# Attention over inducing points with a two-layer block: another order of the last 760 plan tokens, and the last three groups' stores joined

## The chip, the cores and the metric

The kernel runs on one core of a Trainium2 chip. The metric is the device time of one execution in microseconds; three runs of the kernel before gave a median of 542.07 us (541.64 to 542.36).

## The reference

```python
# B, N, m, C = 4, 12480, 32, 128; inducing: (32, 128); d_ff = 2048; float32 in and out
def mab(q, kv):
    s = (q @ kv.transpose(0, 2, 1)) / sqrt(C)
    a = exp(s - s.max(-1, keepdims=True))
    a /= a.sum(-1, keepdims=True) + 1e-09
    return a @ kv

h = mab(I, x)            # 32 inducing points attend to 12480 rows, per batch
y = mab(x, h)            # each row attends to the 32 points
t = y.reshape(B * N, C) @ w_in                              # (49920, 2048)
g = maximum(t, 0) + alpha * minimum(t, 0)
out = g @ w_out                                             # (49920, 128)
```

## The kernel before

The rows of a batch are cut into 24 groups of 512 and a last one of 192; four batches give 100 groups, numbered 0 to 99. Since `y` is a weighted sum of 32 rows of `h`, the first layer is folded into `hW = h @ w_in`, which has only 32 rows. TensorE's array is used as four row tiles of 32 rows (`r` = 0 to 3), which work at the same time.

For a group there are three kinds of work on TensorE (all issued at L383):

- 16 **fills** (`fill`): 32 rows of `hW` times the weights `rep` of the group's tokens into a PSUM bank. Each is then evicted with a ReLU to bf16 (`gt`) by ScalarE (L750, ACT) or VectorE (L752, DVE). A group of 192 tokens has 8 fills of two matmuls each, evicted 384 columns wide.
- the **second** layer (`second`): 16 chunks of `gt` times `W1`, each either as four quarters, one per row tile, or as one **whole** matmul over all 128 rows. All accumulate in one bank.
- one `linear` matmul that opens that bank (`enter`).

When the last chunk is in, `finish` has VectorE transpose the bank into `ot` (L818), multiplies it by the softmax's reciprocal sums (`scaled`, L826, on POOL, that is GpSimd; on VectorE for the very end) and stores `ob`: four stores per group, one for each 32 of the 128 output columns, each 512 pieces of 128 bytes (L851). Their queue depends on `to_end`, the number of groups that end later: four on SyncE for 3, four on ScalarE for 2, mixed for 1 and 0, else all on GpSimd.

The order of everything on TensorE, and with it the order on the evicting engines, is written out by hand in the string `PLAN`, 8041 tokens. A letter `a` to `h` with a bank number is a fill: two letters per row tile, the first evicted by ScalarE, the second by VectorE (`a`, `b` for r = 0, up to `g`, `h` for r = 3). `w`, `x`, `y`, `z` are the next quarter of the second layer in row tile 0, 1, 2, 3; `v` is a whole matmul (for groups 97 to 99 alone); `l` and `m` with a bank open an accumulation for quarters and for whole ones; `s` stands for the remaining work between (scores, sums), with its banks. Instructions go to each engine in the order of the tokens (`pin` ties each to the one before on its engine). A bank is filled again only when it was evicted, and a chunk waits for its `gt`.

Before, the groups at the end finish in the order 95, 97, 98, 96, 99. The last of ScalarE's 78 evictions in the final 760 tokens stands 103 tokens before the end; the 48 whole matmuls stand in three runs of 16.

Of the kernel before, what the change touches and what calls it, by code (L numbers as in the profile page):

```python
# [200 lines left out]
b02h12c223a312s4h212b012a323c12313f413s23e01h112l2wg42d33w231w3e03w32d1w31we431w3f31w3e01w32w3d1  # L201
2w3c42w32wd3g02w132w12h1wc4232xa02h3xa523x23b4x23a1x23xl0w23wxxwf3g5xw3e4s1h5xe3wxe4w3xwf13xw23x
wxe3wh5x2w32wc43wyd13wyc6wg3ys5b4yya1d6ywya5yyg3xb43xy3ya1xyxh6yc53yxh3ya4x3xy3xb1xza6zl5xe7zwxf
3zwc4wzwf1zxwe6zwh7xwzc3wzxwg4d1wzxwe6xzwf7zwzc3ywywzd4ywzc1yzl6yxwg7yxg3wxywh4xywxya1xywxyh2a7x
ywxyb3xya4xywd1ywxe2wxzf7s342zf1xwzxwe3zxwf7zwc2zwyc4zwyd1zwyzyc3zyxb7zyxg2yxb4zyxza1yxzyxb3ze7x
zyxl2yxwg4yxwyxwg1yxwh3yxwxg7wf4xzwxe0zwze1wzywd3zywzyc7wzyd4wzyc0wzwf1zwyza3yza7xyzb4xyza0xzyxl
1zyxwyxwg3yxwh7xywg4yxwh0xywg5xwzxe3wxzwf7xzwxze4wxf5zwc0zwzd3yws745d0wzywyzc3b7yzyzxa4yzxl5yzxb
0yzxa3yzxwzxywxg7ywxg4ywyxh0wyg3xwyxwyxh7wxe6wxzf4wxze0wxze3wzwd7zywc6zywzywd4zyc0zyxb3zyxzya7xz
yb6xzya4xzyl0xzywxg3ywxzywxg7ywxyh6wxywg4xe3wxzwxf2zwxzwe7xzwe4d6zwyzwyd3zwyzc2wyzd7wyza6yzl4xyz
wxyg3b2xyzxwyza6xyzb7xyzwxyg3wxyg2wxyh6ywxwxwxe7zs312xzb7e6xzwf3xzwe2xzwzwc1zywd6yzwc7yzwd2yzwza  # L210
3yzyb1xyzxa6zyxl7zyxwh2yxa3yxzwyxwg6yxwg1yxwyxwh3yxwg2xwe6xwzf5xwzxwze1xwzf3c2wzwzywd6yzwc5yzyzd
1yzb3xyzxa2yzxa6yxzl5yxzwyxza1yxzwyxg2wyxh3wyxg6wyxwyxh1wxe0wxze2wxzwxf3zwze6wzywzyc0wzyd1wzywc2
zyd3l6zyxwzya0xzyb1xzywxzya2zxyzxwys3012xh4ywxg3ywxywh0xywg2xe1wxwzf4xwzxwe3zxwzf2xwzc0wzd1wyzwy
c4zyza3yzxb2yzxl0yzxwyzc1b4yzxwyzxa3yzxwyg2xwyxwh1yxg4wyxwyxg3wyd7wxwe2zxwf1zxwzxwe4zxwf3zc7wzc2
ywzyd1zyxzya4xzb3yxza7yxzyxb2zyxzl1yxg4wyxwh3yxwg7yxzwyxzwyc2ywxg4yxwf3xwze7xwzxwf2s5437wyzd2wyz
c5wyzwyzd4we3zwyzb7yza2yzxya5zxyb4zxyl3zxywxzf7a2xzywxzywxg5ywxg4ywxyh2wxg7wxwxzf5wxze6wxze4wxzw
zd2wzywzc7ywzd6ywzyc5za4yzb2xyzxyl7zxywzxyb6g5xywzxywzxya4xywg2xywh6xywxywg5xwf4xwze0xwzf2xwze6x
wzwzd5ywzc4ywzc0ywzyl6zd2wzyxwzyxzya4xzyb5xzya0xzywxg2ywxzywxywh4xywg5xywxyg0wxs2154wxe0zwxf2zwx
e1zxwze4d5zwzywd0zywc2zyl1yzxwyzxa5zyxb4zyxwyzc2b0yzxwyzxa5yxwzyxwg4yxwg2yxwh0yxwyxwg5xwf4xzwe3x
zwxzwf2c0zwzd5ywyzwyzc4l3yzwxzya2xzyb0xzywxe5zwd4yzwxzya2xzywxzya0xywxh5ywxg4ywxywxg2ywxh0wxe7zw  # L220
xf4zwxzwe5c2zwyzwd0yzl7ywzxya4xzf5wzxywyzc2b0yzxwyzxa4yzxb5yzxwzyc2wzyxs0452ywxg0f6wxg4ywxg5ywxh
2ywxs0d6we4zxwzxwze5xwzf2c0wzd4zyl6yxzwxyza5xyzb2xyzwc0yzwxyzb4xyza5xyzwxyza2xyzwxywg0xyh4wxyg5x
wys21045wxywxh2e1wxf4zwc5zwyzwyc0zwyd1zwyc2zyzb5xyza4xyzl0xyzwxyza1xf2zwxzywxf4g5wxyzwxyza1xzywx
yg2wxyg5wxyh4wxwxf1zwxe3zwzwc2yzwyd5wzyc4wzyzl3d1yzwxyza2xyzwxf5zwxe4zwxyzb1xyza2xywzxyzwc5ywxyg
4wxyg1b2xywxywxe5b7xzwe4xzwd2zwxe1zwd5zwyc7zwyzc4yb2zxyl1zxywzxya5h7yxwzyxwg4d2ywzywxza5yxzyb7xz
xywg4ywxzywxg2yxwe5wxf7wzxf4xzws2657wxzf2wzc4wzyd6wzyc7l5zywwzxywwwzxe2b4zxywwzxywa7h6xywwxzywwx
zwe2wb4xyzwxwzya7xzyl6xywxg2ywxyh4wxywg7xywxwf0c2zwyxzxwxyxh4wc7yzxwyxzxwxe2d0zwyxzxwyxzwc7f4zxw
yxzxwyc2zb0yxzxxyza7xyzb4xyzxya2zxyzl0xywg7xywxyh4ywyxe2zwxyzwyxyyh3we7xzwyxyzywyxe4h2wxyzwyxyyz
wyc7f3zwyzwyc4zwyd2zwyzwc7yzyb3zxya4zxyzxa2yzxl7yzxzwyzzxa3zf4zxzwzyzxzwzyg2xywh1xwyzxg3wyxzzwxz
ze4wzxf2wzxwe1zxwzf3c5wzywzyc4wzyd2wzyc1zwyb3zyza5xyzxyb4zxya2zxyl1xzywxze3xwyh5xwyg4xwyxwyg2xwy  # L230
h3s6452xzwf3xzwe6xzwe4xzwf2xzwc5zwzwyd3wzywd6zywc4zya2zyl5zyxwh3yxwzyxwg4yxb6zyxwzyxa2yzxwyxwyg3
xwyxh4ya6xwe2xwxzf0wxzwxe3zwxzf6wzc4wzywd2zywc0zyzya3zxb6yzxyl4zxywzc2b0yzxywzxya3zxywg6xywxyh2w
xywg0xyg3wxywh7xwe6xzwxzwf2xzwe0xzwd3zwyzc7wyzwyza6d2yzl0xyzwxyg3wd7yzwxyzwxe6zb2xyzwxyza3xyzwxy
a7xywh6xyg2wxywxyg3wxf1wxwzxe7wzxf2zwc6zwyzwd3yzc1yzxa7yzxb2yzxl6yzxwyzc3b1yzxwyzxwyg7xb2yzxwyzx
we3zwxyg1wxywxywxh7ys23517xwzf2xwze3xwzf7c5wzwzyc1wzyd2wzya3zyzyxb7zyxa5zyxb1zyxl2zyxwze3xwzyd7w
yxg5wyxzwyxg1wyxg3wyxh7wyxwxg5wxzf1wxze4wxzwzd3wzyc7wzyd5wzyc1l4zyxwzyxa3zf7xwzyxwze1xzb5yxzwyxz
a3yxzwyxg7wyxwh1yxa5yxwg3yxwyxh0wyxwe7xwzf5wc1zywzywd3zywc0zya7zyxb5zyxl1zyxwzyc3b0zyxwzyxwg7f5x
wzyxwzyxa3zf0xwzyxwg7yxwzyxwg5yxwf3xwe0zxwzxwze7wd6zywzywc5yzd0l3zwxe7zwxzyb6xzywc5yzwxyzxb0yzxa
7zyxwyh6xa5yzxwyzxwyg0xwyxwg7yxwyh5xws60275h6we0xwzxwzd2e5zyc7wzywzyd0l6zyxwzyxa5zyd2wzyxwg7yxwz
f0xwzyxa5zyxwh2yxwze7xwzyxwh0yxa5yzxwyxza2yxg7wxwzxf0wze5wzywd2zywc4zya7zyxzb0yxzl5yxzwyxg2b4yxz  # L240
wyxzwyc7h0wyxzwyxza2yxh4wyxzwyc7zwyxzwe0xwf2zxwzxe4wzxwzxe7wzd0wzywzc1yl4zd2ywzxya7zxywh0xywzc1y
wzyxb2zyxa7zyxwzyxa0zyxwg1yxwyxwh2yxwg7yxwxf0we3xzwf1xzwze2xwzwzc7wyzd0yl3zwyxzya2xh1ywxzxya7zxy
b0zxywzc2wyzd1wyzxa7yzwxyzwxyg0wxyh2xwyg1wxye7wxwxzf0s6127f0zxwe6zxwzd1we7zwyzc2yzxyb0zxyzxya6zy
xb7zyxa1zyxl2zyd0wzyxwg6yxwh7yxwzyc1wzyxwg0yxwh6xywxwe7xzwxe1zwxzwf0c5zwyzwd7yzwc6yzwd1yza0yzxl5
yzxwyzxa7f6zxwyzxwyg0xb1yzxwyzxa7yzxwyg6xwyh0xwyxg1wyxwe7xwzxf4wzxe6wzwzyd1wzyc0wzyd7wzya4zya6xz
yxzb1yxzl0yxzwyd7zwe4xzwyxzwe6xzwyxg1wyxwh4yxwyg7xwyxh6wyxa3xe1wzxwzf4xwze7wzywzd3ywzc6yl1zyxwh4
yxwg7yxwzyxb3zyc6wzyxwzyxa4h7yxwzyxwzyd3a6zyxwzyxwg4yxwzxe7wzxwzxb6s34273e6wzd4f7wzxe2wzxs3yc6wz
# [60 lines left out]
def kernel(  # L308
# [815 lines left out]
```

## Time and profile before

| | |
|---|---|
| runs | 542.36, 541.64, 542.07 us; median 542.07 |
| profiled execution, first to last instruction | 540.4 us |
| median of the runs less that span | 1.7 us |
| busy: PE, DVE, ACT, POOL | 526.3, 504.2, 496.3, 394.7 us |
| mean granted TensorE clock | 0.996 |

The page gives the span of one profiled execution; the time of that execution outside its span is not on it, so times of the profile are set against the runs by these 1.7 us. PE is TensorE, DVE VectorE, ACT ScalarE, SP SyncE. Matmuls of different row tiles overlap, so that PE's busy time is that of at least one tile. Lines are those of the kernel before.

### The profile page before, as it was taken

The numbers are of one execution on the slowest core, as the hardware profiler recorded it, in microseconds if no ns is written. First come the engines' busy times: TensorE is split into PE (matmuls) and PEld (weight loads), VectorE is DVE, ScalarE is ACT, GpSimd is POOL, SyncE is SP. The second block draws the span as 40 slices with busy tenths as digits, with TensorE's granted clock in tenths as the row PEclk, the third lists the DMA queues.
The fourth block names the chain that finished last, engine by engine and source line by source line (L and its number), as shares of the span: only waits on it lengthen the run. The fifth ranks groups of instructions, "written<-read, shape, count | busy, mean of one in ns | idle before, by whom it ended". The sixth has DMA issues, their size and how long they took to land.

```text
span 540.4 us, 21603 instructions
## 1 busy us (share of the span) xinstructions
PE 526.3 (97%) x8988; PEld 332.7 (62%) x8988; DVE 504.2 (93%) x865; ACT 496.3 (92%) x994; POOL 394.7 (73%) x574
## 2 busy tenths in 40 slices
PE   4999999999999999999999999999999999999996
PEld 4655566566567566666667666666666566666653
DVE  3699999999989999999998999999999999999994
ACT  2499999999989999999999999999999999999950
POOL 5553778687667987687687987776767876776764
PEclk9999999999999999999999999999999999999998
DMA  8999999987799898887799797864354344334324
GB/s 197 212 186 139 182 185 156 170 142 113 112 175 149 134 160 152 162 129 145 117 153 166 117 164 158 168 101 113 66 93 113 66 96 112 70 89 108 68 42 85
DMA packets 114738, 71.12 MB, mean 132 GB/s; under 512 B 86784, under 2 KB 102784, under 8 KB 114640
## 3 DMA queue, kind: packets, MB, share of 16 engines
q0 software_dynamic: 19456, 38.62, 38.9%
q1 hardware_dynamic: 91984, 30.22, 32.9%
q8 instruction: 70, 1.15, 0.9%
q10 hardware_dynamic: 3200, 0.90, 0.7%
q14 instruction: 28, 0.23, 0.2%
HBM read 41.00 MB, written 28.95 MB: 129 GB/s over the span
## 4 chain that ended last, share of the span: by engine, by line
PE 90%; DMA 4%; DVE 2%; ACT 1%; POOL 1%; issue 1%; SPq 0%; POOLq 0%; DVEq 0%
PE bank L383 90%; DMA xn<-in_x_dram 2%; DMA rep<-e2d 1%; ACT gt L750 1%; DVE gt L752 1%; DMA e2d<-e 1%; POOL xn L412 0%; DVE ot L818 0%; PE bank L458 0%; ACT e L656 0%; DVE xT L461 0%; POOL ob L826 0%; DVE fr L608 0%; SPq L671 0%; POOL out_dram L851 0%
## 5 line engine op out<-in xcount | busy, mean ns | idle before, releaser
L383 PE MATMUL bank<-gt,W 32*128 32x512 bf16 (+1 forms) x6256 | 480.3, 371 | 0.1
L750 ACT ACTIVATE gt<-bank 128x512 bf16<-128x512 f32 (+1 forms) x906 | 464.5, 612 | 6.9 <-PE bank L383 4.6
L752 DVE TENSOR_SCALAR gt<-bank 128x512 bf16<-128x512 f32 (+1 forms) x662 | 417.7, 677 | 9.9 <-PE bank L383 6.1
L383 PE MATMUL bank<-rep,hW 32*128 32x512 bf16 (+1 forms) x1600 | 418.4, 368 | 1.5 <-DMA rep<-e2d 1.3
L383 PEld LDWEIGHTS <-W 32*128 32x128 bf16 x6256 | 264.4, 92 | 146.5 <-issue 46.6
L851 POOL DMA_DIRECT2D out_dram<-ob x386 | 247.3, 669 | 37.7 <-POOL ob L826 30.4
L826 POOL TENSOR_TENSOR ob<-ot,rdT 128x512 f32<-128x512 f32 (+2 forms) x99 | 106.3, 1074 | 93.8 <-DVE ot L818 79.5
L383 PEld LDWEIGHTS <-hW 32*128 32x128 bf16 x1600 | 136.9, 92 | 20.8 <-issue 5.1
L818 DVE STREAM_TRANSPOSE ot<-bank 128x512 f32<-128x512 f32 (+1 forms) x100 | 69.9, 699 | 6.7 <-PE bank L383 5.6
L383 PE MATMUL bank<-rep,hA 32*128 32x512 bf16 (+1 forms) x100 | 36.1, 367 | 0.0
L427 POOL DMA_DIRECT2D xn<-in_x_dram x32 | 20.7, 663 | 0.1
L481 ACT ACTIVATE e1t<-bank 128x256 bf16<-128x256 f32 (+2 forms) x14 | 5.0, 356 | 10.8 <-PE bank L383 10.8
L461 DVE COPY xT<-bank 128x1024 bf16<-128x1024 bf16 (+1 forms) x13 | 8.5, 650 | 4.9 <-PE bank L458 4.4
L383 PE MATMUL bank<-xT 32*128 32x512 bf16 x81 | 12.5, 376 | 0.0
L553 ACT ACTIVATE e<-bank 128x512 bf16<-128x512 f32 x18 | 11.0, 610 | 0.2 <-PE bank L383 0.2
L656 ACT ACTIVATE e<-bank 128x512 bf16<-128x512 f32 x18 | 11.1, 614 | 0.1
L383 PEld LDWEIGHTS <-xT 128*128 128x128 bf16 (+1 forms) x177 | 8.0, 97 | 4.1 <-issue 1.5
L383 PEld LDWEIGHTS <-hT 128*32 128x32 bf16 (+1 forms) x122 | 3.6, 93 | 11.0 <-issue 10.9
L383 PE MATMUL bank<-xT,hT 128*32 128x512 bf16 (+1 forms) x98 | 10.3, 388 | 0.0
L383 PEld LDWEIGHTS <-hA 32*128 32x128 bf16 x100 | 9.2, 92 | 1.8 <-issue 0.6
L458 PE MATMUL bank<-ident,xn 128*128 128x128 bf16 x96 | 9.0, 249 | 1.0 <-DVE xn L963 0.9
L412 POOL DMA_DIRECT2D xn<-in_x_dram x11 | 6.2, 583 | 3.3 <-DMA xn<-in_x_dram 2.5
(87 smaller groups left out, 131.7 us busy)
## 6 DMA issues: line engine op xcount, KB each, us to landing
out_dram<-ob POOLq DMA_DIRECT2D x373, 64.0 KB, 3.2
rep<-e2d SPq DMA_DIRECT2D x92, 128.0 KB, 3.2
xn<-in_x_dram POOLq DMA_DIRECT2D x37, 256.0 KB, 5.5
e2d<-e SPq DMA_DIRECT2D x24, 128.0 KB, 3.6
xn<-in_x_dram POOLq DMA_DIRECT2D x4, 512.0 KB, 8.2
rdT<-rt SPq DMA_DIRECT2D x96, 8.0 KB, 2.6
early<-in_moe_w_out_dram POOLq DMA_DIRECT2D x4, 256.0 KB, 10.6
xT<-xn SPq DMA_TRANSPOSE x36, 5.2
```

The source lines that it names most:

```text
L383: return pin(nc.tensor.matmul(o, lhsT, rhs, start=start, stop=stop, **kw))
L412: pin(nc.gpsimd.dma_start(out=xn[:, q0:q1, :], in_=src[:, q0:q1, :]))
L427: pin(nc.gpsimd.dma_start(out=st.xn[u][:, part, :], in_=src[:, part, :]))
L458: pin(nc.tensor.transpose(tp[:, k * P : (k + 1) * P], xn[:, q, j * C : (j + 1) * C], ident[:]))
L461: pin(nc.vector.tensor_copy(out=st.xT[:, u, qs[0] : qs[-1] + 1, :].rearrange("c q t -> c (q t)"), in_=tp[:, : len(qs) * GRP],))
L553: pin(nc.scalar.activation(out=e1[:], in_=ps[:], func=EXP, scale=scale, accum_out=st.es[:, u : u + 1]))
L656: pin(nc.scalar.activation(out=e2[:].rearrange("p (t j i) -> p t j i", j=n, i=32), in_=turned(ps[:pp, :w], n), func=EXP, scale=scale_of(st ...
L750: pin(nc.scalar.activation(out=gt[:, :w], in_=ps[:, :w], func=RELU))
L752: pin(nc.vector.tensor_relu(gt[:, :w], ps[:, :w]))
L818: pin(nc.vector.transpose(out=ot[:, :t], in_=acc[:, :t]))
L826: pin(engine.tensor_tensor(out=ob[:, k0 * w : k1 * w].rearrange("p (k m c) -> p k m c", k=k1 - k0, c=32), in0=ot[:, k0 * w : k1 * w].rearr ...
L851: pin(queue.dma_start(out=dst[a], in_=ob[32 * a : 32 * a + 32, :t].rearrange("p (b k) -> p b k", k=32),))
```

## The change

The first 7282 tokens keep their kinds and order; bank numbers differ in 1293 of them. The last 760 tokens stand in another order: 88 evictions are ScalarE's and 62 VectorE's (before 78 and 72), fills go on until 15 tokens before the end, and the whole matmuls are spread over 13 runs among the quarters. The number of matmuls of each kind is the same. The last groups finish in the order 94, 97, 95, 98, 96, 99.

`finish` stores differently for the last three groups (98, 96, 99; `to_end` 2, 1, 0). Group 98 has one store on ScalarE, group 99 one on SyncE. Group 96's first half is multiplied on GpSimd as before; its second half, on VectorE, and its two stores, on ScalarE and SyncE, are held back until group 99 has been multiplied and stored. The group with `to_end` 3 stores on GpSimd.

```diff
-        if to_end == 0:
-            scaled(nc.vector, 0, nb)
-        elif to_end == 1:
-            scaled(nc.gpsimd, 0, nb // 2)
-            scaled(nc.vector, nb // 2, nb)
-        else:
-            scaled(nc.gpsimd, 0, nb)
...
-        queues = {
-            3: (nc.sync,) * 4, 2: (nc.scalar,) * 4,
-            1: (nc.sync, nc.scalar, nc.gpsimd, nc.sync),
-            0: (nc.scalar, nc.gpsimd, nc.scalar, nc.sync),
-        }.get(to_end, (nc.gpsimd,) * 4)
-        for a, queue in enumerate(queues):
-            pin(queue.dma_start(
-                out=dst[a],
-                in_=ob[32 * a : 32 * a + 32, :t].rearrange("p (b k) -> p b k", k=32),
-            ))
...
+        def store(*queues):
+            n = NQ // len(queues)
+            for k, queue in enumerate(queues):
+                pin(queue.dma_start(
+                    out=dst[n * k : n * k + n],
+                    in_=ob[32 * n * k : 32 * n * (k + 1), :t].rearrange("p (b k) -> p b k", k=32),
+                ))
+
+        def rest():
+            scaled(nc.vector, nb // 2, nb)
+            store(nc.scalar, nc.sync)
+
+        if to_end == 0:
+            scaled(nc.vector, 0, nb)
+            store(nc.sync)
+            for fn in held:
+                fn()
+        elif to_end == 1:
+            scaled(nc.gpsimd, 0, nb // 2)
+            held.append(rest)
+        else:
+            scaled(nc.gpsimd, 0, nb)
+            store(*((nc.scalar,) if to_end == 2 else (nc.gpsimd,) * 4))
```

The address patterns of the stores in the built programs (partitions or outermost steps first, last number in elements of 4 bytes):

```
before, each quarter:        ob 32 x 16 x 32   ->  out 512 x 1 x 32   (group 99: 32 x 6 x 32 -> 192 x 1 x 32)
after, group 98 (ScalarE):   ob 128 x 16 x 32  ->  out 4 x 512 x 32
after, group 99 (SyncE):     ob 128 x 6 x 32   ->  out 4 x 192 x 32
after, group 96 (both):      ob 64 x 16 x 32   ->  out 2 x 512 x 32
```

The plan's end, from the first whole matmul on, before and after:

```
before  v*16 yd2m6h7yh1d5 v*16 zzd3m4zzzzzf2zzzzb7f1b5zzzzz v*16
after   vva6zyxxyyh4zzxxe2vvvf5xzzzxa4xa6vvb7yzzyyg2va4yyzc5yzh6vvvva2yzzzyyd7yh4vvc6zyzyzzyyvv
        m5zyzye7h2e4zvvvvvd6zzzze1f7vvvvc4zzzvvvc0h1b2zb6e7zg4vvvvm1zzzvvvve2zzzvvvvvvvvvvvv
```

More of the change, by code (lines that the diff above doesn't have):

```diff
@@ L206 @@
[L206 to L235, printed above, removed]
@@ L304 @@
+yywzzc2ywl0d1zwxyzxwze5yxzyb3yyzc2wxb1yxyzza5wzxyyd3zxzyxxa2wywyxwxwxyg1g5wxwh3s21zwzwxwxxe4zwf5e3wd
+2ywyyc1zyzyc4xyxzb5xyzl3xzwa2h1wxzxyyyxzyxwa4xyyzh5wwg2yxzwxxa1wzh4zxyzxe5yzxwwwxwwc2zze1ys4yzwwyd5z
+yc6wzzzywzyd2c4xh1xyxg5yyxzxyyxyza6zzxxxze2b4m1yg5vva6zyxxyyh4zzxxe2vvvf5xzzzxa4xa6vvb7yzzyyg2va4yyz
+c5yzh6vvvva2yzzzyyd7yh4vvc6zyzyzzyyvvm5zyzye7h2e4zvvvvvd6zzzze1f7vvvvc4zzzvvvc0h1b2zb6e7zg4vvvvm1zzz
+vvvve2zzzvvvvvvvvvvvv
 """
@@ L807 @@
     ended = [0]
+    held = []
     def finish(st, g, acc):
@@ L818, in finish @@
         pin(nc.vector.transpose(out=ot[:, :t], in_=acc[:, :t]))
-        ob = ob_pool.tile([P, GRP], f32, name="ob", tag="ob")
         to_end = B * NG - 1 - ended[0]
         ended[0] += 1
-        def scaled(engine, k0, k1):
-            w = t // nb
-            part = rbc[:, k0:k1]
-            pin(engine.tensor_tensor(
-                out=ob[:, k0 * w : k1 * w].rearrange("p (k m c) -> p k m c", k=k1 - k0, c=32),
-                in0=ot[:, k0 * w : k1 * w].rearrange("p (k m c) -> p k m c", k=k1 - k0, c=32),
-                in1=part, op=MULT,
-            ))
-        if to_end == 0:
-            scaled(nc.vector, 0, nb)
-        elif to_end == 1:
-            scaled(nc.gpsimd, 0, nb // 2)
-            scaled(nc.vector, nb // 2, nb)
-        else:
-            scaled(nc.gpsimd, 0, nb)
         t0 = st.b * N + s * SUP
@@ L844, in finish, with scaled @@
             dst = out[t0 : t0 + REM, :].rearrange("(i b) (a k) -> a i b k", b=t // 32, k=32)
-        queues = {
-            3: (nc.sync,) * 4, 2: (nc.scalar,) * 4,
-            1: (nc.sync, nc.scalar, nc.gpsimd, nc.sync),
-            0: (nc.scalar, nc.gpsimd, nc.scalar, nc.sync),
-        }.get(to_end, (nc.gpsimd,) * 4)
-        for a, queue in enumerate(queues):
-            pin(queue.dma_start(
-                out=dst[a],
-                in_=ob[32 * a : 32 * a + 32, :t].rearrange("p (b k) -> p b k", k=32),
-            ))
+        w = t // nb
+        ob = ob_pool.tile([P, GRP], f32, name="ob", tag="ob")
+        def scaled(engine, k0, k1):
+            pin(engine.tensor_tensor(
+                out=ob[:, k0 * w : k1 * w].rearrange("p (k m c) -> p k m c", k=k1 - k0, c=32),
+                in0=ot[:, k0 * w : k1 * w].rearrange("p (k m c) -> p k m c", k=k1 - k0, c=32),
+                in1=rbc[:, k0:k1], op=MULT,
+            ))
+        def store(*queues):
[19 more added lines that the diff above has]
+            store(*((nc.scalar,) if to_end == 2 else (nc.gpsimd,) * 4))
         st.rep.pop(g)
```

167 lines of the change are left out of this document (94 added, 73 removed).

## The prediction

> **What bounds the kernel now.** I read the page first, then busy time by stretches of the tail, then the timeline of each engine there, then the stores.
>
> ```profile
> span 540.4 us, 21603 instructions
> PE 526.3 (97%) x8988; PEld 332.7 (62%) x8988; DVE 504.2 (93%) x865; ACT 496.3 (92%) x994; POOL 394.7 (73%) x574
> ...
> ACT  2499999999989999999999999999999999999950
> ...
> q10 hardware_dynamic: 3200, 0.90, 0.7%
> ...
> PE 90%; DMA 4%; DVE 2%; ACT 1%; POOL 1%; issue 1%; SPq 0%; POOLq 0%; DVEq 0%
> ```
>
> ```profile
> 505.00:510.00 5.00, 5.00 (x90) 2.88 (x86) 4.85 (x9) 5.00 (x11) 2.91 (x5) 1.00 0.29 60
> 515.00:520.00 5.00, 5.00 (x69) 2.78 (x67) 5.00 (x9) 5.00 (x11) 3.02 (x6) 1.00 0.28 50
> 520.00:525.00 5.00, 5.00 (x36) 2.27 (x31) 4.46 (x8) 0.26 (x1) 2.36 (x4) 1.00 0.29 56
> 525.00:530.00 5.00, 5.00 (x37) 2.25 (x37) 3.42 (x7) 0.00 (x0) 4.28 (x6) 1.00 0.26 52
> 530.00:535.00 5.00, 5.00 (x34) 2.96 (x31) 3.60 (x7) 0.00 (x0) 1.94 (x2) 0.72 0.60 102
> 535.00:540.40 5.40, 0.75 (x5) 0.39 (x3) 0.74 (x2) 0.00 (x0) 1.19 (x2) 0.82 0.40 70
> ```
>
> Columns: stretch, length, then busy time and instructions of PE, PEld, DVE, ACT, POOL, then clock, DMA share, GB/s. Up to 520 DVE and ACT are full and PE too, but PE's 5.00 is a union over four row tiles and hides gaps in one of them. After 520 ACT does nothing, DVE evicts the last groups alone, and PE runs 36 matmuls in 5 us instead of 90: whole ones and lone ones. The span closes with 4.6 us in which PE is done and output travels. So the change works on some 20 us of PE tail and on that end.
>
> **The tail's sum.** Counted on the plan, both orders hold the same 150 fills, 548 quarter matmuls and 48 whole ones in the last 760 tokens. Before evicts 78 on ACT and 72 on DVE, after 88 and 62. The durations:
>
> ```profile
> 508.05 12.21 ACT L750 ACTIVATE gt<-bank 128x512 bf16<-128x512 f32 x24
> ...
> 501.73 0.72 DVE L818 STREAM_TRANSPOSE ot<-bank 128x512 f32<-128x512 f32 x1
> 502.37 5.18 DVE L752 TENSOR_SCALAR gt<-bank 128x512 bf16<-128x512 f32 x8
> 507.47 0.70 DVE L818 STREAM_TRANSPOSE ot<-bank 128x512 f32<-128x512 f32 x1
> ...
> 521.07 3.99 PE L383 MATMUL bank<-gt,W 32*128 32x512 bf16 x18
> ...
> 528.34 1.13 PE L383 MATMUL bank<-gt,W 128*128 128x512 bf16 x4
> ...
> 529.31 0.81 PE L383 MATMUL bank<-gt,W 32*128 32x512 bf16 x3
> 529.75 0.33 PE L383 MATMUL bank<-rep,hW 32*128 32x192 bf16 x2
> 529.96 1.02 PE L383 MATMUL bank<-gt,W 32*128 32x512 bf16 x4
> ...
> 532.49 3.27 PE L383 MATMUL bank<-gt,W 32*128 32x512 bf16 x17
> ...
> 479.30:533.20 53.90, 43.60 (x72) 0.99 0.34 71
> ```
>
> An ACT eviction takes 12.21/24 = 0.509 us; one of DVE (507.47 - 502.37)/8 = 0.6375, a transpose 0.64 to the next start. A matmul of 512 columns takes (3.99 - 0.37)/17 = 0.213 of its row tile, whole or quarter, one of 192 columns 0.08 by width. The last row says that DVE's last 72 evictions start at 479.3: the tail begins there, and its last matmul ends at 532.49 + 3.27 = 535.76, 56.5 us later.
>
> I add up each engine's work to a place in the plan. Before, at the 145th fill: DVE 67 evictions (62 full, 5 of 384 columns at 0.5) and 10 transposes, 48.7 us with its small ones; PE's fullest row tile 41.7 of its 49.8. Evictions lead by 7.0, so PE ends at 49.8 + 7.0 = 56.8; 56.5 was measured. After, at the 140th fill: ACT 41.7, DVE 43.4, PE 42.8. The widest lead is at the 120th: DVE 36.4 against 32.8, 3.6; PE in all 49.7. That gives 53.3, less the 0.3 by which this overshoots before: 53.0.
>
> Against it: the 48 whole matmuls stand in 3 runs before and 13 after. The row of four at 528.34 shows the price of leaving a run: 1.13 - 0.38 - 2 x 0.213 = 0.32 to the next start instead of 0.213, so 0.1; the way in is not separable in a row, I take 0.1 as well. Ten more runs cost 2.0 (bounds 0, where evictions are late anyway, and 2.0): 55.0. The plan's ragged places (four w, then four x) cost little: the fill at 529.75 stands in the plan behind seven z, of which one ended the row at 528.34 and three the row at 529.31; three follow only from 529.96. So PE lets a matmul overtake three of another row tile.
>
> **ACT's queue.** The store of group 98, the third from last, now stands in ACT's queue ahead of the last eviction of group 99, for which the last two whole matmuls wait. It waits for DVE's transpose and POOL's product:
>
> ```profile
> 525.91 2.57 POOL L851 DMA_DIRECT2D out_dram<-ob  x4 [0.30 <-POOL ob L826]
> ...
> 529.26 0.72 DVE L818 STREAM_TRANSPOSE ot<-bank 128x512 f32<-128x512 f32 x1 [1.41 <-PE bank L383]
> ...
> 530.06 1.07 POOL L826 TENSOR_TENSOR ob<-ot,rdT 128x512 f32<-128x512 f32 x1 [0.48 <-DVE ot L818]
> ...
> 535.86 0.38 DVE L818 STREAM_TRANSPOSE ot<-bank 128x192 f32<-128x192 f32 x1 [1.46 <-PE bank L383]
> 536.28 0.36 DVE L826 TENSOR_TENSOR ob<-ot,rdT 128x192 f32<-128x192 f32 x1
> ...
> L851 SPq DMA_DIRECT2D out_dram<-ob x7: 571/627/737, 529.6 to 536.7; - x7
> L851 ACTq DMA_DIRECT2D out_dram<-ob x7: 581/651/871, 531.2 to 537.3; - x7
> ...
> DMA to landing us min/median/max: 1.9/2.2/2.4
> ```
>
> From group 98's last whole matmul: 0.5 to the transpose, 0.72, 0.08, 1.07, 0.1, issue 0.65, eviction 0.45, so 3.6 us. PE meanwhile has six z (1.3), fourteen whole ones of 192 columns (1.1) and five switches (0.5): 2.9. The stall is 0.6 (0 if z run late; 2.6 if issuing four times the rows takes 4 x 0.65). PE ends at 479.3 + 55.0 + 0.6 = 534.9, 0.9 earlier. Bounds: 3.5 earlier with switches and stall hidden, 1.5 later. The half clock seen in the last stretches I leave as it is; gone, it gives back about 1 us, inside these bounds.
>
> POOL takes four more stores, group 97's, which SP issued before: product, gap and stores are 1.07 + 0.30 + 2.57 = 3.9, for groups 97 and 95 together 7.9 from 1.3 after group 97's end, so until 9.2; group 98's transpose is done 7.7 + 1.3 = 9.0 after that end (6.7 of matmuls on the fullest tile, five switched runs). POOL is free just in time; 0.2 more at worst lies inside the bounds.
>
> From there to the last issue: before 537.3 - 535.76 = 1.5. After: transpose, product of group 99, then DVE's half product of group 96, which now waits behind them (`held`), with gaps 1.35, and SP is busy with group 99's store to 1.5. Equal, nothing gained. Issues saved (12 stores become 4) cost nothing: SP and ACT had nothing else behind them.
>
> **The joined stores.** This decides.
>
> ```profile
> 530.50:531.00 0.50, 0.50 (x10) 0.31 (x8) 0.18 (x1) 0.00 (x0) 0.50 (x1) 1.00 0.01 2
> 531.00:531.50 0.50, 0.50 (x6) 0.21 (x3) 0.38 (x1) 0.00 (x0) 0.13 (x1) 1.00 0.75 130
> 532.50:533.00 0.50, 0.50 (x2) 0.00 (x0) 0.50 (x2) 0.00 (x0) 0.00 (x0) 0.50 1.22 198
> ...
> 539.00:540.40 1.40, 0.00 (x0) 0.00 (x0) 0.00 (x0) 0.00 (x0) 0.00 (x0) 0.50 0.02 3
> ...
> q10 hardware_dynamic: 3056, 0.38, 19.9%
> ...
> SPq L1119 <- DMA out_dram<-ob: 1.7, 2, 1.4
> ```
>
> A store of one quarter is 512 pieces of 128 B. Over 529 to 540.4 ACT's queue (q10) took 0.199 x 16 x 11.4 us for 3056 packets: 11.9 ns each on its engine. One queue alone moves 130 GB/s, 128 B per engine in 15.8 ns; two together 198, 10.3 ns. At 198 GB/s all sixteen engines must be at work. Every hardware transfer of this kernel has 16, 32, 96, 128, 192 or 512 as the outermost count of both its patterns; page q10's 3200 are 2944 pieces, 128 packets of the first load and 8 x 16 closing ones, so each was dealt over sixteen engines. The joined stores are the only ones with an outermost count of 4 (groups 98 and 99) or 2 (the two halves of group 96). If a transfer is dealt by its outermost count, these run on 4, 4, 2 and 2 engines. No row shows such a count, so the price is bounded: at least nothing (dealt over sixteen), at most everything on the same engines one after another. I take the latter's place, since a whole outermost step per engine is the plainest dealing that the rows allow, and there is no other reason for each to close with sixteen.
>
> The Trainium skill (DMA: Bandwidth & Descriptors, "Why a DMA increments its semaphore by 16 and not by 1") says that: the number of engines is the largest up to 16 that divides the outermost non-unit size of both patterns, and ScalarE's and SyncE's transfers take the lowest-numbered ones. By it the sum is the one below; no run here shows it yet.
>
> Per engine then: group 98 512 pieces, group 99 192, each half of group 96 512. If all share the first two engines, 1728. Group 98's last matmul is 3.6 before PE's end, its issue 2.5 after that, first pieces 1.4 after the issue (529.6 to 531.0 above): 534.9 - 3.6 + 2.5 + 1.4 = 535.2. ACT's queue is alone for 2.5 us (158 pieces at 15.8); then SP's 704 pieces and as many of ACT's alternate at 10.3 each, 14.5 us; the 162 left take 2.6. That is 19.6 us, to 554.8. From the last piece (539.1) to the end it was 1.3: span 556.1. The median lies 542.07 - 540.4 = 1.7 above the profiled span: 557.8. Bounds: all at 10.3, 17.8 us, with PE 2.6 earlier still, 553.4; all at 15.8, 27.3 us, 565.5.
>
> **Rivals.** (1) Few engines, but different ones for each store: the last store starts at 536.3 + 1.4 and takes 512 pieces at 11.9 to 15.8, 6.1 to 8.1: 546.8 to 548.8. For it: nothing in the rows says that engines repeat. (2) Faster: the joined stores are dealt over sixteen engines like the rest; then the end is as before and only PE's gain is left: 542.07 - 0.9 = 541.2, and 538.6 with the switches and the stall hidden. For it: all rows so far have sixteen. It decides as soon as group 98's store moves at 130 GB/s. (3) PE issues strictly in order: counted on the plan, a round opened whenever a row tile repeats, the tail takes 72 us after against 52 before, so 562 even with sixteen engines; the overtaking at 529.75 speaks against it.
>
> **How the numbers follow.** All few-engine stores on the same engines 0.62, rival 1 0.18, rival 2 0.18, rival 3 0.02. A change within 0.2% (1.1 us) can't be told from none. Rival 2's 538.6 to 543.6 falls 0.11 faster, 0.05 same, 0.02 slower. Predicted 557.8; the range 545 to 565 holds the first case and rival 1. Faster 0.11, same 0.05, slower 0.84.
>
> **What would show it.** Page part 3: q10 has 3072 + 128 pieces and 16 + 4 + 2 closings, 3222, by few engines, and 3248 by sixteen. The last fifteen microseconds show a DMA share near 2/16 and some 25 GB/s with all engines idle, and the chain's DMA share grows from 4% to about 7%. PE's last matmul lies at 534.9. ACT still evicts until about 532. Wrong would be a landing of the joined stores near 2.2 us, or a PE tail over 57.

## The result, and the profile after

The changed kernel takes 570.75 us (median of four, 569.65 to 571.71), before 541.86: ratio 1.0535, 95% interval [1.0517, 1.0553]. The forecast was 557.8 in 545 to 565: the right sign, and 13 us too little. The page of the changed kernel:

```profile
span 568.8 us, 21597 instructions
PE 534.8 (94%) x8985; PEld 331.5 (58%) x8988; DVE 502.0 (88%) x855; ACT 504.0 (89%) x1004; POOL 396.8 (70%) x576
...
ACT  2599999999999999999999999999999999888510
...
q10 hardware_dynamic: 3222, 0.92, 0.8%
...
PE 51%; POOL 25%; issue 12%; DMA 4%; DVE 1%; SPq 1%; ACT 1%; POOLq 0%; ACTq 0%; DVEq 0%
```

ACT's row ends in 888510 where before had 999950: in its last slices ScalarE is less full than before. q10 has the 3222 packets that were forecast for few engines. Stretches (length, busy time and instructions of PE, PEld, DVE, ACT, POOL, then clock, DMA share, GB/s):

```profile
505.00:510.00 5.00, 5.00 (x72) 2.73 (x70) 4.35 (x7) 4.60 (x10) 3.31 (x5) 1.00 0.26 54
515.00:520.00 5.00, 4.78 (x77) 3.34 (x79) 3.89 (x7) 4.32 (x10) 3.36 (x5) 1.00 0.33 66
...
530.00:535.00 5.00, 4.84 (x39) 1.52 (x36) 2.57 (x4) 2.19 (x4) 1.48 (x3) 1.00 0.27 56
...
545.00:550.00 5.00, 0.33 (x2) 0.10 (x1) 1.14 (x3) 0.49 (x1) 0.47 (x1) 0.83 0.21 32
550.00:555.00 5.00, 0.00 (x0) 0.00 (x0) 0.00 (x0) 0.00 (x0) 0.00 (x0) 0.50 0.37 41
555.00:560.00 5.00, 0.00 (x0) 0.00 (x0) 0.00 (x0) 0.00 (x0) 0.00 (x0) 0.50 0.21 22
560.00:565.00 5.00, 0.00 (x0) 0.00 (x0) 0.00 (x0) 0.00 (x0) 0.00 (x0) 0.50 0.21 22
```

Two things are to be seen. From 550 on every engine is idle and output trickles, at 41 and then at 22 GB/s: the joined stores, as forecast. But in 505 to 510 PE ran 72 matmuls where before ran 90, and ACT and DVE have gaps too. Nobody is full: they wait for each other. The end in the timeline (start, length, engine, line, then in brackets what the first of the group waited for):

```profile
541.22 2.57 POOL L838 DMA_DIRECT2D out_dram<-ob  x4 [0.96 <-POOL ob L829]
...
541.90 0.72 DVE L815 STREAM_TRANSPOSE ot<-bank 128x512 f32<-128x512 f32 x1
...
543.72 1.75 POOL L829 TENSOR_TENSOR ob<-ot,rdT 128x512 f32<-128x512 f32 x2
...
544.92 1.16 ACTq L838 DMA_DIRECT2D out_dram<-ob  x1
546.21 0.49 ACT L746 ACTIVATE gt<-bank 128x384 bf16<-128x384 f32 x1 [4.70 <-POOL ob L829]
546.75 0.33 PE L379 MATMUL bank<-gt,W 128*128 128x192 bf16 x2 [2.08 <-ACT gt L746]
```

PE's last matmul ends at 546.75 + 0.33 = 547.08 instead of 534.9. From there to the end of the span it is 21.8 us, forecast 21.2. So 12.2 of the 13 us of the miss lie in PE's tail.

To find it I cut that tail, from the start of its first fill, at the start of the last fill up to token 7900. Up to there lie 598 to 606 fills and quarters on the plan (600 before, 601 after; eight more or less are 0.4 us at 0.213 us for four), and the first whole one comes later. All profiles of the old order left as it was give 36.9 us for this **first part**, those of the new one 45.0, whatever else differs. The **second part** runs from there to PE's end. (The tail itself starts between 477.6 and 481.7 us in these profiles, whatever the order, so its length is compared and not its place.)

The last two columns are about waits. A **hand-over** is the place where a row tile begins its quarters of a group: all four row tiles add into one bank, and the first quarter of a row tile waits for the last one of the row tile before. How many tokens lie between a step and what it waits for I call its slack. The columns sum over the records of the first part: for each TensorE instruction with a semaphore wait, the time since the start of the TensorE instruction before it, as far as it is over 0.1 us; at the weight loads that wait for a hand-over, and at fills that wait for a bank.

```
order and stores                          first  second  hand-overs  fills
before                                     36.9    20.1      0.4      0.5
after                                      45.0    22.8      2.6      2.0
new order alone (e1)                       45.0    23.4      2.6      2.0
new order, row tiles alternating (e4)      42.6    23.1      2.9      3.8
new order, quarters and fills moved (e7)   39.1    23.6      0.3      1.2
  and group 98 stored by SyncE (e11)       39.1    19.5
new order, all mended (e10)                39.0    19.4      0.6      2.2
new order, five hand-overs wider (e9)      44.6    23.2      2.1      2.1
new order, no runs of three (e14)          43.9    23.6      1.0      1.8
new order, fills moved alone (e15)         42.4    23.9      1.3      2.6
old order made ragged (e5)                 39.6    18.5      0.9      3.1
old order, hand-overs tight (e12)          41.0    20.5      5.3      0.7
old order, runs of three (e13)             40.6    18.4      0.4      1.8
old order, evictions shared (e8)           36.9    20.3
```

### The profile page after: what moved, and what is told of

It is laid out like the page before. It is cut to its first block, busy times and chain, and to the rows that moved or that the text cites. A ratio compares the mean times of both kernels' runs of the same rounds, so it can differ in the third digit from the quotient of the medians.

```text
span 568.8 us, 21597 instructions
## 1 busy us (share of the span) xinstructions
PE 534.8 (94%) x8985; PEld 331.5 (58%) x8988; DVE 502.0 (88%) x855; ACT 504.0 (89%) x1004; POOL 396.8 (70%) x576
## 3 DMA queue, kind: packets, MB, share of 16 engines
q10 hardware_dynamic: 3222, 0.92, 0.8%
## 4 chain that ended last, share of the span: by engine, by line
PE 51%; POOL 25%; issue 12%; DMA 4%; DVE 1%; SPq 1%; ACT 1%; POOLq 0%; ACTq 0%; DVEq 0%
PE bank L379 51%; POOL out_dram L838 17%; POOL ob L829 8%; DMA xn<-in_x_dram 2%; DMA rep<-e2d 1%; DVE gt L748 1%; ACT gt L746 1%; DMA rdT<-rt 1%; SPq L667 0%; POOL xn L408 0%; SPq L707 0%; PE bank L454 0%; SPq L428 0%; DVE xT L457 0%; DVE fr L604 0%
## 5 line engine op out<-in xcount | busy, mean ns | idle before, releaser
L746 ACT ACTIVATE gt<-bank 128x512 bf16<-128x512 f32 (+1 forms) x916 | 471.9, 608 | 25.6 <-PE bank L379 17.7
L379 PE MATMUL bank<-gt,W 32*128 32x512 bf16 (+2 forms) x6253 | 488.2, 371 | 3.1 <-ACT gt L746 2.1
L423 POOL DMA_DIRECT2D xn<-in_x_dram x32 | 20.7, 663 | 0.1
L379 PE MATMUL bank<-xT,hT 128*32 128x512 bf16 (+1 forms) x98 | 10.3, 388 | 0.0
```

What stands on the lines that cost most here:

```text
L379: return pin(nc.tensor.matmul(o, lhsT, rhs, start=start, stop=stop, **kw))
L423: pin(nc.gpsimd.dma_start(out=st.xn[u][:, part, :], in_=src[:, part, :]))
L746: pin(nc.scalar.activation(out=gt[:, :w], in_=ps[:, :w], func=RELU))
```

## The experiments

**e1: the order alone.** Edit: the new `PLAN` in the kernel before, whose `finish` stays.

> The new order of the 760 tokens with the stores of before (four a group, queues by to_end as before). In the changed kernel PE's last matmul ends at 547.1 instead of 535.8 us and the end behind it takes 21.7 instead of 4.6 us. Theory: the two parts are separate; the order alone costs the 11 us of PE, 551 to 555 us. Rival: PE's delay is made by the joined stores (ScalarE held behind POOL and its store); then the order alone gives 541 to 545 us.

Measured: 554.2 us, ratio 1.0226 [1.0196, 1.0256]. Its tail is 68.4 us, its end 4.6 us behind PE as before. So the order alone costs 12 us where the forecast had it gain 0.9.

**e2: the stores alone.** Edit: the old `PLAN` with the new `finish`.

> The order of before with the new finish (joined stores, held half). Theory (joined stores run on 4, 4, 2 and 2 engines, the first ones each time): 557 to 561 us, q10 3222 packets, about 22 GB/s in the last stretches. Rival (the stores are late only because PE is late): 541 to 544 us.

Measured: 559.56 us, ratio 1.0325 [1.03, 1.0351]. PE ends at 533.3, the span at 557.7. The page's q10 and stretches of it:

```profile
q10 hardware_dynamic: 3222, 0.92, 0.8%
...
540.00:545.00 5.00, 0.00 (x0) 0.00 (x0) 0.00 (x0) 0.00 (x0) 0.00 (x0) 0.50 0.33 37
545.00:550.00 5.00, 0.00 (x0) 0.00 (x0) 0.00 (x0) 0.00 (x0) 0.00 (x0) 0.50 0.21 22
550.00:555.00 5.00, 0.00 (x0) 0.00 (x0) 0.00 (x0) 0.00 (x0) 0.00 (x0) 0.50 0.21 22
```

The same 22 GB/s without the new order. The two parts of the change nearly add: 2.3% and 3.3% against 5.4% together.

**e3: joining alone.** Edit to the changed kernel: four stores per group again, on the same queues.

```diff
-            for k, queue in enumerate(queues):
-                pin(queue.dma_start(
-                    out=dst[n * k : n * k + n],
+            for a in range(NQ):
+                pin(queues[a // n].dma_start(
+                    out=dst[a],
```

> The changed kernel with four separate stores per group (512 pieces each, outermost count 512 as before) on the same queues and in the same order as the changed kernel's joined ones, group 96's half still held back. If the joined access pattern is what costs (few engines), the end is again some 5 to 7 us behind PE and the time is that of the new order alone, 553 to 557. If the queues chosen or the held half cost, it stays at 563 to 571.

Measured: 559.1 us, ratio 1.0299 [1.0259, 1.0339], between the two expectations and some 2 to 6 us over what the first gave. Joining costs 1.0535 - 1.0299, or 2.4% (13 us); the choice of queues and the held half, together, are not free either: the span ends 7.7 us behind PE instead of 4.6. And four issues in ScalarE's queue hold the last eviction longer than one joined store does:

```profile
544.96 2.72 ACTq L838 DMA_DIRECT2D out_dram<-ob  x4
547.81 0.49 ACT L746 ACTIVATE gt<-bank 128x384 bf16<-128x384 f32 x1 [6.24 <-DMA out_dram<-ob]
548.35 0.48 PE L379 MATMUL bank<-gt,W 128*128 128x192 bf16 x2 [3.63 <-ACT gt L746]
```

3.63 us of stall instead of 2.08: here the joined issue gave back 1.5 us.

**e8: evictions shared, nothing else.** Edit: the old `PLAN`, seven of the last 15 evictions given to ScalarE by their letter (the lines show the fills alone).

```diff
-h5 h2 b6 d7 h1 b5 d2 h7 h1 d5 d3 f2 b7 f1 b5
+h5 g2 b6 c7 h1 a5 d2 g7 h1 c5 d3 e2 b7 e1 b5
```

> The old plan and the old stores; of the last 15 evictions, all VectorE's, every second one (7) is ScalarE's. It does alone what the change says of the evictions (both engines evict to the end). By the prediction's sum evictions led PE by 7.0 us there, and 7 x 0.64 = 4.5 us leave VectorE: 537 to 539. If PE's fullest row tile sets the end there (its matmuls with the closing linear ones are about 52 of the 56.5 us), nothing comes: 541 to 542.

Measured: 542.83 us, ratio 0.9999 [0.998, 1.0019]. Nothing comes. Its stretches show both engines at work from 520 on and neither full, while PE nearly is:

```profile
520.00:525.00 5.00, 4.84 (x45) 2.51 (x42) 4.30 (x8) 3.46 (x7) 3.85 (x6) 1.00 0.25 55
525.00:530.00 5.00, 5.00 (x32) 2.23 (x31) 1.76 (x3) 0.87 (x2) 4.12 (x6) 1.00 0.27 54
530.00:535.00 5.00, 5.00 (x34) 2.07 (x33) 2.36 (x5) 0.00 (x0) 1.07 (x1) 0.88 0.41 71
```

A stretch in which TensorE's clock is granted at 0.50 (the half clock below) falls into the second part before as well as here, with a mean of 0.92 and 0.91, so it hides no gain. These seven evictions were not late. The expectation's 52 us count the `linear` matmuls to the fullest row tile; but they open the banks, in row tile 0, and row tile 3 counts 49.8 us as in the prediction. What supports the expectation's argument is the second part: row tile 3 has 17 us of matmuls left there on the plan, and at full clock the old order takes 18.4 to 18.5 (e2, e5, e13), so little room is left for waiting.

**m1: TensorE by itself.** Edit: behind the end of the kernel before, bursts of matmuls are added: 96 quarters in runs of one to four and of eight per row tile; whole ones alone and in turn with four quarters; ten fills, each behind three quarters of three other row tiles, then ten behind four quarters of one, each with an eviction by ScalarE. Its time includes that added work.

> Kernel before with matmuls added behind its end, which nobody reads: 96 quarters in runs of 1, 2, 3, 4 and 8 per row tile (24 a tile, 5.1 us if the tiles overlap fully), whole ones alone and each followed by four quarters, and ten fills with an eviction on ScalarE, behind three quarters of other tiles or behind four of one tile. Theory A (TensorE issues nearly in the plan's order): the runs of 2, 3, 4 take about 10, 14 and 15 us. Theory B (it overtakes at least three, as a row of before showed): runs up to 3 take 5 to 6 us, runs of 4 up to 8, but an eviction behind four quarters of one tile starts 0.4 to 0.6 us later after its fill's start than one behind three different tiles, because it waits for the matmuls in front of the fill as well.

Measured, groups of instructions (busy time, mean ns of one) for runs of one (L1102), two (L1104), three (L1106), four (L1108) and eight (L1110), and whole ones alone (L1116):

```profile
L1110 PE MATMUL bank<-xT,W 32*128 32x512 bf16 x96 | 11.6, 375 | 0.0
...
L1108 PE MATMUL bank<-xT,W 32*128 32x512 bf16 x96 | 5.4, 374 | 0.0
L1102 PE MATMUL bank<-xT,W 32*128 32x512 bf16 x96 | 5.3, 374 | 0.0
L1104 PE MATMUL bank<-xT,W 32*128 32x512 bf16 x96 | 5.3, 374 | 0.0
L1106 PE MATMUL bank<-xT,W 32*128 32x512 bf16 x96 | 5.3, 374 | 0.0
...
L1116 PE MATMUL bank<-xT,W 128*128 128x512 bf16 x16 | 3.6, 380 | 0.0
```

Strictly in order, runs of four would take 24 x 3 x 0.2135 = 15.4 us. They take 5.4, hardly more than runs of one with 5.3: overtaking is free up to four deep, where no instruction waits, and at eight the time doubles. The Trainium skill (TensorE: Matmul & The Clock Gate, "Part 3: Packing small matmuls — row/col tiling") says that matmuls start and end strictly in program order; these starts do not. Whole ones alone follow one another at 0.216 us; four quarters and one whole matmul in turn had a period of 0.65 = 2 x 0.216 + 0.22, so a switch costs 0.11 each way, against 0.1 in the forecast. And the evictions:

```profile
579.76 0.37 PE L1140 MATMUL bank<-xT,W 32*128 32x512 bf16 x1
...
580.22 0.60 ACT L1141 ACTIVATE gt<-bank 128x512 bf16<-128x512 f32 x1 [61.13 <-PE bank L1132]
...
586.28 0.38 PE L1147 MATMUL bank<-xT,W 32*128 32x512 bf16 x1
...
587.36 0.60 ACT L1148 ACTIVATE gt<-bank 128x512 bf16<-128x512 f32 x1 [0.27 <-PE bank L1134]
```

Behind three quarters of three row tiles the eviction starts 0.46 us after its fill (L1140), behind four of one row tile 1.08 us (L1147), 0.62 later where 0.4 to 0.6 was expected: the fill overtakes three of the four, but its eviction waits until they are done too. The bracket names them, L1134, as what it waited for. In the records the last of the four and the fill count up the same semaphore, for whose value the eviction waits; whether a semaphore of its own would release it earlier, no run shows.

**e4: row tiles alternating.** Edit: tokens of the new order shifted within eight places so that row tiles take turns; stores of before.

```diff
- y y c7 y z w w d3 z z c5 x l1 y x z y z w d2 x y
+ z y w d3 y z w c5 y z x z l1 y x w z y d2 a7 z x
```

> The new order with only quarters and fills moved past one another within eight tokens, so that a row tile seldom repeats before the others had a turn: counted in strict order the tail takes 55 us of matmuls instead of 73 (54 before). Fills keep their order, engines and banks; whole matmuls stay where they are; stores of before. Theory (runs of one row tile in the plan cost the 11 us): 540 to 545 us, DVE and ACT full again until about 520. Rival (the spread whole matmuls and the later evictions cost it): 549 to 555 us.

Measured: 551.53 us, ratio 1.0179 [1.0153, 1.0205]. Only 2.7 us come back, which is in the rival's range. The rival's reason is not what is left, though: the first part ends ahead of the first whole matmul and still takes 5.7 us more than the old order's. It falls to 42.6, but its waits grow from 4.6 to 6.7 us: in moving tokens, I brought six hand-overs as near as 2 tokens and fills nearer to the evictions that free their banks.

**e5: the old order made ragged.** Edit: tokens 7282 to 7840 shifted by three places at most so that row tiles repeat.

```diff
- z y d1 w z y c2 z y x z b6 y x z a0 y x z l7 y x
+ c7 d1 y y w z z c2 x y y z z b6 a0 x x y z l7 z y
```

> The old plan and the old stores, with tokens 7282 to 7840 made as ragged as the new plan (row tiles repeat two and three at a time; the same count of rounds, 73 us against 54), each token moved by three places at most; hand-overs stay 4 to 5 tokens at the least. Theory R (raggedness): 8 to 12 us slower than before, 550 to 554. Theory S (slack): little is lost, since overtaking covers runs of up to four: 541.5 to 545.

Measured: 544.88 us, ratio 1.0039 [1.0015, 1.0062]; first part 39.6. That is theory S's range. Raggedness, mostly by twos, still costs 2.7 us in the first part, and the waits at fills grow by as much, 0.5 to 3.1. On the plan this order has as many strict rounds as the new one.

**e7: slack mended.** Edit: the new order with its quarters and fills moved against each other for distance; the fills keep their own order, banks and engines. (The whole matmuls came to stand in six runs by this, not in thirteen as the expectation has it.)

```diff
- y y c7 y z w w d3 z z c5 x l1 y x z y z w d2 x y
+ d3 c5 z z w y z y y z y x d2 z y a7 z x z l1 w y
```

> The new plan with the four-per-group stores of before (as in the run of the order alone, 554.2), in which only quarters of the last 760 tokens have moved against the fills and whole matmuls; the fills keep their order, banks and engines, the whole matmuls their 13-odd places. Every first quarter of a group in a row tile now stands at least 5 tokens behind the last one of the row tile before (2, 2, 3, 4, 4 at the least before the edit, 5 in the kernel before), and a fill stands further behind the use that frees its bank. The tokens stay ragged: opening a round whenever a row tile repeats counts 68 us of it (73 in the new plan, 54 in the old). Theory S (missing slack: the instruction that waits for a hand-over or for a bank holds up all four row tiles): nearly all of the 12.7 us comes back, 540 to 545. Theory R (raggedness or spread whole matmuls themselves cost): most stays, 550 to 554.

Measured: 548.89 us, ratio 1.0106 [1.0079, 1.0133]; between the two theories' ranges; first part 39.1, so 5.9 of its 8.1 us are back. Slack was not all that changed: from token 7282 to 7900 the same row tile still comes twice or more in a row at 85 places where the new order has 100, but three times or more at 4 where it has 23. The stretch 479 to 500 before, after and in e7:

```profile
479.00:500.00 21.00, 21.00 (x363) 13.09 (x360) 20.95 (x36) 20.99 (x42) 15.67 (x22) 1.00 0.36 86
```

```profile
479.00:500.00 21.00, 20.63 (x294) 10.40 (x292) 17.57 (x29) 17.50 (x34) 12.66 (x18) 1.00 0.31 72
```

```profile
479.00:500.00 21.00, 21.00 (x338) 13.62 (x334) 20.17 (x33) 19.93 (x39) 14.66 (x21) 1.00 0.36 84
```

363, 294 and 338 matmuls; DVE and ACT go from 17.5 back to 20. The second part did not shorten, which left the stall at the end as a suspect.

**e11: the store out of ScalarE's queue.** Edit to e7:

```diff
-            3: (nc.sync,) * 4, 2: (nc.scalar,) * 4,
+            3: (nc.sync,) * 4, 2: (nc.sync,) * 4,
```

> The new plan with the slack mended (548.9, ratio 1.0106), and group 98's four stores on SyncE instead of ScalarE; nothing else. If the last eviction queued behind these stores in ScalarE's queue holds TensorE up at the end (one wait of 2.8 us there), 2 to 3 us come back: ratio 1.005 to 1.007. If the last fills are late anyway, nothing: 1.010.

The waits, e7 ahead of e11 (total, times, longest):

```profile
ACT gt L746 <- DMA out_dram<-ob: 5.8, 1, 5.8
...
PE bank L379 <- ACT gt L746: 2.8, 1, 2.8
```

```profile
PE bank L379 <- issue: 0.3, 2, 0.2
```

PE's wait for ScalarE is gone, and the second part falls from 23.6 to 19.5 (some of that is e7's half clock behind the wait). But the time is 546.68 us, ratio 1.0104 [1.0076, 1.0132], no better than e7's: SyncE now issues 11 stores one after another, and the end comes 5.9 us behind PE instead of 4.7. In the time itself the expected 2 to 3 us cannot be shown: the profiled spans are 546.8 and 545.0.

**e9, e14, e15: which slack?** Three edits to the new order, each aimed at one thing. e9 widens the five tightest hand-overs to 5 tokens (15 tokens differ). e14 lets quarters trade places until no row tile comes three times in a row. e15 moves fills alone.

```diff
e9
- z w z z w x f2 y
+ z w x z z w f2 y
e14
- y y c7 y z w w d3 z z c5 x l1 y x z y z w d2 x y
+ y z c7 w z y w d3 y z c5 x l1 y y w x z z d2 y x
e15
- y y c7 y z w w d3 z z c5 x l1 y x z y z w d2 x y
+ x c5 y y y y z d2 w w z a7 z x l1 y x z y a3 z w
```

> The new plan with the stores of before (the order alone measured 1.0226 of before, 12.3 us), with one thing mended: quarters next to the five tightest hand-overs are shifted by one to three places, so that no first quarter stands nearer than 5 tokens behind the last one of the row tile before (2, 2, 3, 4, 4 before the edit); 15 tokens differ. If the tight hand-overs were most of the missing slack, the first part of the tail loses 3 to 6 us of its 8 and the time is 547 to 551. If the slack is missing between fills, evictions and banks, 0 to 1.5 us come back: 552.5 to 554.

> The new plan and the old stores; in tokens 7282 to 7900 quarters trade places among themselves so that no run of three or more of one row tile is left (23 before); the fills keep their places, and hand-overs are as near as they were (3, 3, 4, 4, 5 at the least). Theory Q: the tail's first part, 45.0 us in the new order, becomes 40.5 to 42, the time 549 to 552. Theory W: it stays within 1 us, 44 to 45 and 553 to 555.

> The new plan and the old stores; only fills move: 121 of the 150 in the last 760 tokens stand elsewhere among the quarters (2.2 tokens earlier on average), while the fills among themselves and the quarters and whole matmuls among themselves keep their order exactly. So hand-overs stay as near (2, 2, 3, 3, 4 at the least) and row tiles repeat as often. Theory F (the new order asks for banks too soon: a fill that waits for its bank holds everything behind it, and that delays the next eviction in turn): the tail's first part, 45.0 us in the new order, falls by 3 to 4.5 us, the time to 549 to 551.5. If hand-overs and runs of one row tile are what costs, at most 1 us comes back: 553 to 555.

Measured ratios: e9 1.0245 [1.0218, 1.0271], e14 1.022 [1.0202, 1.0238], e15 1.0163 [1.0116, 1.0209]. First parts: 44.6, 43.9, 42.4. The edits gave back 0.4, 1.1 (my theory had 3 to 4.5) and 2.6 (3 to 4.5 expected). None alone is the cause; their sum, 4.1, is short of the 5.9 that e7 recovers. Nor is each gain the price of the one thing named: without runs (e14) the waits at hand-overs fell as well, by 1.6, and with the fills moved (e15) the waits at fills grew, 2.0 to 2.6, while those at hand-overs fell, 2.6 to 1.3, and runs of three or more went from 23 to 15.

**e12, e13: the same put into the old order.** e12 draws 22 hand-overs closer, most to 2 or 3 tokens. e13 makes 26 runs of three or four by letting quarters trade places; every fill stays.

```diff
e12
- w z x f0 w z c7 w z y d1 w z y c2 z y x
+ w z x f0 y w z c7 w z d1 w z y c2 x z y
e13
- z y d1 w z y c2 z y x z b6 y x z a0 y x z l7 y x
+ w y d1 w z y c2 z z x y b6 x y y a0 x z z l7 z x
```

> The old plan and the old stores; only first quarters of a group in row tiles 1 to 3 are moved forward, so that 17 of the 26 hand-overs stand 2 or 3 tokens apart and 5 stand 4 or 5 (5 to 9 in the old plan). The rest keeps its order. If a tight hand-over stalls all row tiles for 0.15 to 0.25 us, 22 of them cost 2 to 5 us: 544 to 547. If hand-overs are covered by what row tiles still have queued, 541.5 to 542.5.

> The old plan and the old stores; in tokens 7282 to 7900 quarters trade places among themselves so that 26 runs of three or four of one row tile arise (none before; 23 in the new plan). Every fill, opening and closing token keeps its place, and no hand-over is nearer than 5 tokens. Theory Q (a run of three fills the queue ahead of a waiting instruction and leaves other row tiles empty, some 0.18 us each): the tail's first part, 36.9 us in every run of the old order, becomes 40.5 to 41.5, the time 545 to 547. Theory W (only the waits at hand-overs and fills cost): at most 1.5 us more, 542 to 543.5.

Measured: e12 547.66 us, 1.0103 [1.0084, 1.0122]; e13 545.47 us, 1.0063 [1.0039, 1.0086]. They cost 4.2 and 3.7 us of first part. In e12 the waits at hand-overs go from 0.4 to 5.3 us, about what the first part loses; in these waits no TensorE instruction starts, though quarters of other row tiles stand behind.

**e10: all mended.** Edit: e7's means, with row tiles alternating (54 us of strict rounds, as the old order), hand-overs 6 tokens apart at the least, and group 98 stored by SyncE.

```diff
- y y c7 y z w w d3 z z c5 x l1 y x z y z w d2 x y
+ z d3 w y c5 w z y z y z y d2 z a7 y l1 z x w y y
```

> The new plan's fills in their order, with their banks and engines (88 evictions on ScalarE, to the end), everything else of the last 760 tokens mended at once: hand-overs 6 tokens apart at the least, fills placed for slack, row tiles alternating (54 us of strict rounds as in the old plan, 68 in the run with the slack mended alone), six runs of whole matmuls, and group 98's four stores on SyncE instead of ScalarE, so that the last eviction is not queued behind them. If the four causes (slack 5.9, raggedness about 2, the store in ScalarE's queue about 2.5, switching 1 to 2) are all there is, nothing is left of the 12.3 us: 540 to 543. If spread whole matmuls and late evictions cost by themselves, 544 to 548.

Measured: 547.02 us, ratio 1.0091 [1.0077, 1.0106]. The time lies in the range given to spread whole matmuls and late evictions, but the loss does not lie there: the first part, ahead of them, is 2.1 us longer than before, with 2.2 us of waits at fills left, the second 0.7 shorter, and the end 6.7 us behind PE against 4.6, since the stores now end later. No order tried here beats the kernel before.

## Why the prediction was wrong, by its own steps

The forecast's tail was 55.6 us; 67.8 were measured. The terms:

- **The gain from shared evictions, 3.5 us, did not come** (the step "Evictions lead by 7.0"). The sums by engine compared evictions with 49.8 us of PE and took the difference for lateness. e8 moves 4.5 us of evictions to ScalarE and changes nothing. By the same sums the lead at the 120th fill was 5.0 before and 3.6 after; that part of the gain, 1.4, lies ahead of what e8 moved and no run tests it. Miss 3.5.
- **"The plan's ragged places cost little"** is the step that failed. That TensorE overtakes was right, m1 shows it up to four deep. What was missing is that an instruction with a wait lets nothing pass (e12), and that an eviction is released only when the matmuls ahead of its fill are done as well, 1.08 us instead of 0.46 (m1). The profile of before had it beside the row on which the step rested, in the eviction of the fill of 529.75:

```profile
530.82 0.56 DVE L752 TENSOR_SCALAR gt<-bank 128x384 bf16<-128x384 f32 x1 [0.40 <-PE bank L383]
```

  It starts 1.07 us after that fill, when the three z that the fill had overtaken were done. So a ragged order can be free in matmuls and still cost waits. The first part took 45.0 instead of 36.9. Miss 8.1.
- **The stall in ScalarE's queue**, 0.6, was 2.08. POOL was not "free just in time": group 98's transpose was done at 541.90 + 0.72, its product began behind POOL's stores at 543.72, 1.1 later; and the joined issue took 1.16 instead of 0.65. 0.6 + 1.1 + 0.5 = 2.2. The bound for the issue alone was there; the 0.2 allowed for POOL was not enough. Miss 1.5.
- **Switches**, 2.0: at full clock the old order's second part is 18.4 to 18.5 (e2, e5, e13), the new one's 22.8 less the stall 20.7. Right to 0.2, though other effects of the order may be in it.
- **The half clock** of before (0.72 in the stretch 530 to 535) was absent in PE's tail after, and gives back 20.1 - 18.5 = 1.6; the forecast had left it in place and put it at about 1.

With 0.5 for where the tail is counted from: 55.6 + 3.5 + 8.1 + 1.5 + 0.2 - 1.6 + 0.5 = 67.8.

The **end** was right in its mechanism. The 3222 packets are those of 4, 4, 2 and 2 engines. The rule of the Trainium skill that the forecast named (DMA: Bandwidth & Descriptors, "Why a DMA increments its semaphore by 16 and not by 1") is borne out by them. From 549 to 554, while a store with an outermost count of 4 still runs, 44 GB/s move, and 22 where only those of 2 are left; 22 GB/s on two engines is 11.6 ns for 128 bytes, within the 10.3 to 15.8 used. Against rival 1 speaks that ScalarE's and SyncE's queues together move 22 GB/s from 557 to 564 and SyncE's alone 22 from 565 to 566.5: both stores use the same two engines. Against rival 2 speaks e2. That the size of the end came out within 0.6 us, 21.8 against 21.2, is luck in part: the first packet left 0.8 us before PE's end and not 0.3 behind it, since PE's last matmuls waited behind that store's issue, the packets took 20.8 us and not 19.6, and the close behind them 1.8 and not 1.3. The forecast of a DMA share near 2/16 was off: 0.21, with both queues and with SyncE's alone. In the records a packet then lasts 19.4 ns on average while one per engine leaves every 11.8, so packets overlap. The chain's DMA share stayed at 4%.

Rival 3 (strict order, 72 us of tail) came nearer in size than the forecast, but not in mechanism: m1 excludes it, and e5, with as many strict rounds on the plan as the new order and a tail of 58.1 us. The bounds were too narrow: the row at 529.75 shows that a fill overtakes quarters, and its price was taken from that alone.

**What stays open.** How the 8.1 us split between hand-overs, fills and runs: near hand-overs and runs each cost more in the old order (4.2 and 3.7) than their mending alone gives back in the new one (0.4 and 1.1), and e5, e7, e13, e14 and e15 each moved more than one of them. Where row tiles alternate (e4, e12, e10), what the first part loses equals the growth of the listed waits to within 1.1 us; in the ragged ones, but for e5, about half of it or more stands in no such wait, and I read it as row tiles that run empty behind one. That is argued, not shown.

## What to carry to other kernels

A sum by engine finds the slowest engine, not the price of an order: count for each step that waits how far behind its producer it stands, and what is queued behind it. Before work is moved to an idle engine, move a little of it and look whether the end moves; here a change of seven letters told that the last evictions were not late. Of a store, look at the outermost count of both its patterns before its number of issues.

## What the runs showed of the hardware

- An eviction behind four queued matmuls of another row tile starts 1.08 us after its fill's start, behind three of different ones 0.46, though the fill overtakes three of the four; the last of the queued ones and the fill count up one semaphore here (m1).
- Matmuls of other row tiles are overtaken up to runs of four at next to no cost (96 in 5.4 us, in runs of one 5.3), at runs of eight the time doubles (11.6, all m1).
- Two stores with an outermost count of 2, one on ScalarE's queue and one on SyncE's, together move 22 GB/s, as one of them alone does (after the change, from 557 on).
- Joined stores mostly take their queue longer to issue than single ones did (0.57 to 0.87): group 98's 1.16 us, group 96's two halves, behind other stores in their queues, 3.02 and 4.88, group 99's, of 192 pieces for each of four engines, only 0.73. Shortest, middle and longest in ns:

```profile
L838 ACTq DMA_DIRECT2D out_dram<-ob x2: 1162/2094/3025, 544.9 to 548.6; - x2
L838 SPq DMA_DIRECT2D out_dram<-ob x2: 725/2802/4879, 548.2 to 549.0; - x2
```
